# Merging two inverse spectral branches before their shared inverse stage, with SBUF-to-SBUF transfers that turn the rows

## The chip, the cores and the metric

The kernel runs on one core of a Trainium2 chip. The metric is the device time of one execution, in microseconds (us); lower is better. The engines are called PE (TensorE matmul), PEld (its weight loads), DVE (VectorE), ACT (ScalarE), POOL (GpSimd) and SP (SyncE, which here only issues transfers). A profile is one execution, and its span (first to last instruction) is 1.8 us shorter than the time of the same run.

Each timed run has a state: fast, slow (over 1.5% above the fastest of the same kernel), or unknown (a single run). The only profile of the kernel before is of a 155.47 us run, about 1% above the median, so its stage times are good to about 1%.

## The reference

One input `x` (2048 x 1024, bf16) goes through a real 2-D FFT. Its spectrum is multiplied by two sets of complex weights, A and B. Each product is transformed back, and a per-row gate `g` mixes the two.

```python
def _A_ref(x, w_r, w_i):                 # _B_ref is the same with B's weights
    X = rfft2(x.astype(float32), axes=(-2, -1))
    X = X * (w_r + 1j * w_i)
    return irfft2(X, s=(S, D), axes=(-2, -1)).astype(bfloat16)

x = A_x                                  # B_x is not used
g = sigmoid((x * gate_w).sum(-1, keepdims=True))
return g * a + (1 - g) * b               # a, b: the two branches
```

The 2048 rows are treated as 128 x 16 (n1, n2), so that every transform is a matmul with a constant matrix: along n1 (128 points), along n2 (16 points, "the 16-point stage"), and along the 1024 columns ("over d"). The gate depends on the row alone, so it can be folded into the matrix that undoes n1.

## The kernel before

The kernel is written in the form of units ("U") with a reads list and a writes list; a list scheduler in the same file orders them with estimated costs and puts in the semaphore waits. `EV` is an eviction, which copies a PSUM slot (128 x 1024) to SBUF and goes to ACT or DVE, whichever the scheduler thinks is done first.

The stages are: fold of x by symmetry (DVE), forward n1 (PE), gate row (PE), forward over d (PE), forward 16-point stage (PE), then for each branch eight complex products (DVE), the inverse 16-point stage, the inverse over d, and last one mixed inverse over n1, an unfold and a store.

The gate row, whose moving operand is read in runs of 32 elements:

```python
def gate_row(c):
    ops = [mm(misc(0, [[1, 512]], 1), ap(G8, q, [[1, 1]]),
              ap(R3, q * 2048 + c * 32, [[128, 16], [1, 32]]), q == 0, q == 7)
           for q in range(8)]
    ...
```

One product is two multiplies, one subtraction and one addition, for two of the 16 rows kg at once:

```python
def prod(b, m):
    ...
    r = [(tt(ap(RING, TO, ...), x, w, ALU.mult), rd, ["t0"]),
         (tt(ap(RING, TO + 2048, ...), x, ws, ALU.mult), rd, ["t1"])]
    for c, op in enumerate((ALU.subtract, ALU.add)):
        ...
```

The inverse 16-point stage takes the product as the stationary operand, so that the result lands with d on partitions, ready for the inverse over d. That is run once per branch, and each of its 32 results is evicted:

```python
def stage_i1(b, kg):
    ...
    w = ap(PT, p + c * 512 + lb % 2 * 256 + lb // 2, [[2, 128]])       # stationary: data
    r.append(mm(pslot(s, lb * 256, [[1, 256]]), w, ap(KI, z + c * 256, [[1, 256]]), c == 0, c == 1))

def stage_dinv(b, n2):                       # 2 branches x 16 rows n2, 8 matmuls each
    ...
    return U(("di", b, n2), "pe", ops, [("V", b, k) for k in range(16)] + [("Vf", b), "DI"],
             after=[("row", b)] + ([("di", 0, 15)] if b else [("grow", 3)]), slot=True, prio=4,
             then=[lambda s: EV(("evD", b, n2), 1024, dst, pslot(s, 0, [[1, 1024]]), [], w, after=af, slot=s)])

def s1inv(n2):                               # the mixed inverse over n1, from both branches
    ...
```

The weights come in pieces, each for 16 partitions 8g + j, in the order j = 0..3 (`pm` = 0) and then j = 4..7 (`pm` = 1):

```python
for pm in range(2):
    for ii in range(4):
        for c in range(2):
            ...
            prs.append((AP(T, (4 * pm + ii) * P + ..., [[8 * P, 16], [2 * NS, k1 - k0], [1, n]]), ...))
```

Of the kernel before, what the change touches and what calls it, by code (L numbers as in the profile page):

```python
# [10 lines left out]
NS = 514  # L11
PW = 128
# [8 lines left out]
def make_consts():  # L21
# [13 lines left out]
    C["F"] = F.reshape(128, 2048)  # L35
    R = np.zeros((64, 2, 16, 128))
# [4 lines left out]
    C["RM"] = R.reshape(128, 2048)  # L41
# [3 lines left out]
    for h in range(2):  # L45
        d = (h * 128 + np.arange(128))[:, None] + 0.5
        lev, lod = 2 * m, 2 * m + 1
        les = np.where(m == 0, 512, 2 * m)
        DM[:, 0, h] = np.cos(pi2 * lev * d / 1024)
        DM[:, 1, h] = -np.sin(pi2 * lod * d / 1024)  # L50
        DM[:, 2, h] = -np.sin(pi2 * les * d / 1024)
        DM[:, 3, h] = np.cos(pi2 * lod * d / 1024)
# [4 lines left out]
    for par in range(2):  # L57
        for h in range(2):
            l = (2 * (h * 128 + np.arange(128)) + par)[:, None]
            DI[:, par, h, 0] = np.where(l == 0, 1.0, 2.0) / 1024 * np.cos(pi2 * l * d / 1024)  # L60
            li = np.where(l == 0, 512, l)
            DI[:, par, h, 1] = -np.where(li == 512, 1.0, 2.0) / 1024 * np.sin(pi2 * li * d / 1024)
# [3 lines left out]
    KI = np.zeros((2, 2, 128, 2, 16, 4, 2))  # L66
    for z in range(2):
        for pm in range(2):
            for k2 in range(16):
                for ii in range(4):  # L70
# [3 lines left out]
                    for q2 in range(16):  # L74
# [16 lines left out]
                        K = KI[z, :, po, :, q2, i, :]  # L91
# [11 lines left out]
    C["KI"] = KI.reshape(2, 2, 128, 256).transpose(2, 0, 1, 3).reshape(128, 1024)  # L103
# [3 lines left out]
    C["GS"] = np.repeat(gs.reshape(128, 1), 16, axis=1)  # L107
    one = np.zeros((128, 2))
    one[0] = 1.0
    C["ONE"] = one  # L110
    idt = np.zeros((128, 16))
    idt[:16] = np.eye(16)
    C["ID"] = idt
# [13 lines left out]
class Sched:  # L127
# [4 lines left out]
    def __init__(self):  # L132
        self.q = {e: [] for e in self.ENG}
        self.all = []
        self.writer, self.readers = {}, {}
        self.free = {e: 0.0 for e in self.ENG}
        self.dmafree = 0.0

    def ready(self, eng, reads, writes):

        t = self.free[eng]
        for k in list(reads) + list(writes):
            for d in self.writer.get(k, ()):
                t = max(t, d.end + (60 if d.eng == eng else 160))
        for k in writes:
            for d in self.readers.get(k, ()):
                t = max(t, d.end + (0 if d.eng == eng else 160))
        return t

    def op(self, eng, fns, reads=(), writes=(), dma=False, ns=0.0):  # L150
# [10 lines left out]
        for k in writes:  # L161
            o.deps |= self.writer.get(k, set())
            o.deps |= self.readers.get(k, set())
        for k in reads:
# [90 lines left out]
def bass_gated_mix__spectral_gfnet__spectral_gfnet__prompt_kernel(  # L255
# [15 lines left out]
    R2 = sb("R2", 32 * NS)  # L271
    R3 = sb("R3", 16384)
    R4 = sb("R4", 16384)
    R5 = sb("R5", 32 * NS)
    FM = sb("FM", 2048)
    DM = sb("DM", 2048)
    S2 = sb("S2", 768)
    KI = sb("KI", 1024)
    DI = sb("DI", 2048)
    RM = sb("RM", 2048)  # L280
    GS = sb("GS", 16)
    ONE = sb("ONE", 2)
    ID = sb("ID", 16)
    V6 = sb("V6", 256)
    RING = sb("RING", 11264)
    GROW = sb("GROW", 512)
    X5 = sb("X5", 32)
    P5 = sb("P5", 192)
    V5 = sb("V5", 256)
    ZG = sb("ZG", 16)  # L290
    G8 = sb("G8", 8)
# [3 lines left out]
    S = Sched()  # L295
    x2, out2 = A_x[0], out[0]
# [3 lines left out]
    WR = {0: R5, 1: R2}  # L300
    VR = {0: R1, 1: R5}
    QO, TO, PO = 0, 3072, 7168
    VBO, OO, HO, YO = 0, 2048, 4096, 6144
    PSL = [(RING, PO), (RING, PO + 2048), (FM, 0)]

# [6 lines left out]
    def mm(o, l, r, start=True, stop=True):  # L312
        n = int(np.prod(o.shape[1:]))
        return (lambda e: e.matmul(o, l, r, start=start, stop=stop, skip_group_check=True)), max(65.0, 0.42 * n)  # L314
# [13 lines left out]
    class U:  # L328
# [4 lines left out]
        def start(self):  # L333
# [14 lines left out]
            if self.eng == "ev":  # L348
# [3 lines left out]
                return (ta, "act", ca) if ta + ca <= td + cd + (300 if dnext[0] < td + 400 else 0) else (td, "dve", cd)  # L352
# [77 lines left out]
    def cload(eng, t, key, n, alias=(), after=()):  # L430
        return U(("ld", key), eng, [(ap(t, 0, [[1, n]]).bitcast(dt.uint16), cst[key].ap())], [], [key] + list(alias),
# [6 lines left out]
    def wload(b, ka, kb, after=()):  # L438

        prs = []  # L440
        T = WR[b]
        P = pit[id(T)]
        for pm in range(2):
            for ii in range(4):
                for c in range(2):
                    src = wsrc[b][c]
                    n = src.shape[-1]

                    def part(r0, step, k0, k1):
                        prs.append((AP(T, (4 * pm + ii) * P + (2 * k0 + c) * NS, [[8 * P, 16], [2 * NS, k1 - k0], [1, n]]),  # L450
                                    AP(src.tensor, src.offset + (r0 + step * k0) * n, [[128 * n, 16], [step * n, k1 - k0], [1, n]])))
                    if pm == 0:
                        part(16 * ii, 1, ka, kb)
                    elif ii < 3:
                        part(80 + 16 * ii, -1, ka, kb)
                    elif ka == 0:
                        part(128, -1, 1, kb)
                        part(64, 1, 0, 1)
                    else:
                        part(128, -1, ka, kb)  # L460
        return U(("ldw", b, ka), "sp", prs, [], [("W", b, k) for k in range(ka, kb)] + (["gwt"] if b else []),
                 after, dma=(True, 1500.0 * (kb - ka)))

    gwl = U(("ld", "gw"), "act", [(ap(R2, 2048, [[1, 1024]], 0, 1), gate_w.rearrange("(o d) -> o d", o=1))], [], ["gw"],
            dma=(True, 10.0))
    loads = [xload(0, 2), cload("sp", FM, "F", 2048), xload(2, 4), xload(4, 8), xload(8, 12), xload(12, 16),
             cload("sp", DM, "DM", 2048), cload("sp", S2, "S2", 768), cload("sp", KI, "KI", 1024),
             cload("sp", GS, "GS", 16), cload("sp", ID, "ID", 16), wload(0, 0, 8), wload(0, 8, 16),
             wload(1, 0, 16, after=["G8mm"]), cload("sp", DI, "DI", 2048),
             cload("sp", RM, "RM", 2048, ["zrow"], after=["gspec"])]  # L470
# [3 lines left out]
    def fold(name, n, src, soff, tmp, st, dst, doff, p0, np_, reads, skey, writes, eng="dve", after=()):  # L474
# [9 lines left out]
        for i, op in enumerate((ALU.add, ALU.subtract)):  # L484
# [3 lines left out]

    folds = [fold(("fold", m), 2, R1, m * 2048, RING, m % 2 * 2048, R4, m * 2048, 0, 128, [("x", 2 * m), ("x", 2 * m + 1)],
                  ("st", m % 2), [("u", 2 * m), ("u", 2 * m + 1)], after=[("ldx", (0, 2, 4, 4, 8, 8, 12, 12)[m])]) for m in range(8)]  # L490
    gfold = [fold("gfold", 1, R2, 2048, R2, 4096, R2, 3072, 0, 1, ["gw"], ("gst",), [("ug",)], eng="pool", after=[("ld", "gw")])]

    def s1(n2):
        def ops(s):
            return [mm(pslot(s, q * 128, [[1, 128]]), ap(R4, n2 * 1024 + q * 128, [[1, 128]]), ap(FM, n2 * 128, [[1, 128]]))
                    for q in range(8)]
        return U(("s1", n2), "pe", ops, [("u", n2, 0), ("u", n2, 1), "F"], after=[("fold", n2 // 2), ("ld", "F")], slot=True, prio=2,
# [3 lines left out]
    def gate_row(c):  # L501
        ops = [mm(misc(0, [[1, 512]], 1), ap(G8, q, [[1, 1]]), ap(R3, q * 2048 + c * 32, [[128, 16], [1, 32]]), q == 0, q == 7)
               for q in range(8)]
        return U(("grow", c), "pe", ops, ["G8"] + [("Z", 4 * c + i) for i in range(4)], ["m7"], prio=6,
                 after=["G8"] + [("evZ", 4 * c + i) for i in range(4)] + (["x5"] if c == 3 else []),
                 then=[EV(("zrow", c), 512, ap(RM, c * 512, [[8, 16], [128, 4], [1, 8]], 0, 1),
                          misc(0, [[32, 16], [8, 4], [1, 8]], 1), ["m7"], [("zrow", c)])])

    gate = [U("G8mm", "pe", [mm(misc(q, [[1, 1]]), ap(R2, 3072 + q * 128, [[1, 128]], 0, 1), ap(ONE, 0, [[1, 1]], 0, 1))
                             for q in range(8)], [("ug", 0), ("ug", 1), "ONE"], ["m7", "gwt"], after=["gfold", ("ld", "ONE")], prio=6,  # L510
              then=[EV("G8", 8, ap(G8, 0, [[1, 8]]), misc(0, [[1, 8]]), ["m7"], ["G8"])])]
    gate += [gate_row(c) for c in range(4)]
    gate += [U("gspec", "pe", [mm(misc(n2, [[1, 1]]), ap(RM, n2 * 128, [[1, 128]], 0, 1), ap(ONE, 0, [[1, 1]], 0, 1))
                               for n2 in range(16)], [("zrow", c) for c in range(4)] + ["ONE"], ["m7", "zrow"],
# [5 lines left out]
    allu = [("u", m, i) for m in range(16) for i in range(2)]  # L520
# [3 lines left out]
    def stage_d(kg):  # L524
        def ops(s):
            return [mm(pslot(s, o, [[1, 256]]), ap(R3, (2 * g + h) * 2048 + kg * 128, [[1, 128]]),
                       ap(DM, (2 * g + h) * 256, [[1, 256]]), h == 0, h == 1)
                    for g, o in ((0, 0), (3, 256), (2, 512), (1, 768)) for h in range(2)]
        r = kg % 3
        return U(("d", kg), "pe", ops, allz + ["DM"], after=[("evZ", m) for m in range(16)], slot=True, prio=4,  # L530
                 then=[lambda s: EV(("evQ", kg), 1024, ap(RING, QO + r * 1024, [[512, 2], [1, 2], [2, 256]]),
                                    pslot(s, 0, [[512, 2], [256, 2], [1, 256]]), [],
                                    [("Q", r)] + ([("st", i, t) for i in range(2) for t in "ST"] if kg == 0 else []),
                                    after=[("s2", kg - 3)] if kg > 2 else [], slot=s)])

    def stage_s2(kg):
# [3 lines left out]
        def Q(c, a, n):  # L540
            return ap(RING, QO + r * 1024 + c * 512 + a, [[1, n]])

        def ops(s):
# [3 lines left out]
                    mm(pslot(s, 1, [[1, 511]]), Cn, Q(1, 1, 511), False, True),  # L547
                    mm(ap(PS, 3072 + kg, [[1, 1]]), Cn, Q(1, 0, 1)),
                    mm(pslot(s, 513, [[1, 511]]), A, Q(1, 1, 511), False, True),
# [196 lines left out]
```

## Time and profile before

| what | value | from |
|---|---|---|
| time | 154.23 us median (153.45 to 156.2) | three runs |
| span, clock of the PE | 153.7 us, 0.983 | the profiled run |
| DVE / PE / ACT busy | 124.9 / 124.2 / 118.7 us | part 1 of the page |
| first product | 35.72 us | timeline, DVE |
| end of weight traffic | about 68 us | slices, DMA |
| start of branch B's inverse over d | 116.53 us | timeline, PE |
| from there to the end (the tail) | 37.2 us | the same |

The first fence has lines of the profile page of the kernel before: the span, busy time per engine (us, share of the span, instructions), and rows of the span cut into 40 equal slices, in which a digit is the busy share in tenths (the GB/s row is what the transfers moved).

```profile
span 153.7 us, 2554 instructions
PE 124.2 (81%) x1015; PEld 88.4 (58%) x1024; DVE 124.9 (81%) x193; ACT 118.7 (77%) x128; POOL 5.5 (4%) x8
...
DVE  0899998337979989919997996998974699799993
...
PEclk9999999999999999999959999999999999999997
DMA  5899999999999999980000400000000033333253
GB/s 160 272 430 417 307 169 181 177 166 177 175 172 165 164 181 167 167 186 0 0 0 0 138 4 0 0 4 0 0 0 5 0 136 136 136 136 118 95 205 137
```

A slice is 3.84 us. Read the rows by stage. The weights (slices 5 to 17) crawl at about 170 GB/s with the transfer engines full. Almost nothing moves in the middle; stores run at the end. DVE is nearly full from about 35 us on, but for its wait for the last weights in slice 17, and the PE keeps its full clock in all but two slices.

### The profile page before, as it was taken

The numbers are of one execution on the slowest core, as the hardware profiler recorded it, in microseconds if no ns is written. First come the engines' busy times: TensorE is split into PE (matmuls) and PEld (weight loads), VectorE is DVE, ScalarE is ACT, GpSimd is POOL, SyncE is SP. The second block draws the span as 40 slices with busy tenths as digits, with TensorE's granted clock in tenths as the row PEclk, the third lists the DMA queues.
The fourth block names the chain that finished last, engine by engine and source line by source line (L and its number), as shares of the span: only waits on it lengthen the run. The fifth ranks groups of instructions, "written<-read, shape, count | busy, mean of one in ns | idle before, by whom it ended". The sixth has DMA issues, their size and how long they took to land.

```text
span 153.7 us, 2554 instructions
## 1 busy us (share of the span) xinstructions
PE 124.2 (81%) x1015; PEld 88.4 (58%) x1024; DVE 124.9 (81%) x193; ACT 118.7 (77%) x128; POOL 5.5 (4%) x8
## 2 busy tenths in 40 slices
PE   0058897699999999989299599999987999999920
PEld 0057454467686867663168487878876467456400
DVE  0899998337979989919997996998974699799993
ACT  3046889489999899998159689999977789598770
POOL 4900000000000000000000000000000000000000
PEclk9999999999999999999959999999999999999997
DMA  5899999999999999980000400000000033333253
GB/s 160 272 430 417 307 169 181 177 166 177 175 172 165 164 181 167 167 186 0 0 0 0 138 4 0 0 4 0 0 0 5 0 136 136 136 136 118 95 205 137
DMA packets 13422, 19.54 MB, mean 127 GB/s; under 512 B 1761, under 2 KB 10081, under 8 KB 13026
## 3 DMA queue, kind: packets, MB, share of 16 engines
q1 hardware_dynamic: 13264, 19.37, 55.6%
q8 instruction: 8, 0.13, 0.4%
q14 instruction: 4, 0.03, 0.1%
q10 hardware_dynamic: 146, 0.00, 0.1%
HBM read 15.17 MB, written 4.19 MB: 126 GB/s over the span
## 4 chain that ended last, share of the span: by engine, by line
SPq 34%; PE 32%; ACT 10%; DVE 10%; DMA 8%; issue 4%; DVEq 0%
SPq L358 34%; PE PS L314 32%; DVE RING L318 9%; DMA R<-in_B_w_i_dram 8%; ACT R L363 6%; ACT RING L363 3%; DVE FM L318 1%; ACT L363 1%; ACT GROW L363 1%; DVEq L233 0%; DVE P L318 0%; DVE RING L365 0%; DVEq L219 0%
## 5 line engine op out<-in xcount | busy, mean ns | idle before, releaser
L363 ACT ACTIVATE R<-PS 128x1024 bf16<-128x1024 f32 x71 | 68.5, 1030 | 17.2 <-PE PS L314 17.0
L318 DVE TENSOR_TENSOR RING<-R 128x2048 bf16<-128x2048 bf16 (+1 forms) x48 | 49.0, 1062 | 10.7 <-DMA R<-in_A_x_dram 4.3
L363 ACT ACTIVATE RING<-PS 128x1024 bf16<-128x1024 f32 x41 | 43.8, 1131 | 8.3 <-PE PS L314 8.3
L318 DVE TENSOR_TENSOR RING<-RING 128x512 bf16<-128x512 bf16 (+1 forms) x94 | 42.6, 505 | 0.6
L314 PE MATMUL PS<-KI,RING 128*128 128x256 bf16 x240 | 30.4, 279 | 3.1 <-DVE P L318 2.9
L314 PE MATMUL PS<-DI,R 128*128 128x256 bf16 x256 | 30.9, 273 | 1.8 <-ACT R L363 1.8
L314 PEld LDWEIGHTS PS<-DI,R 128*128 128x128 bf16 x256 | 24.2, 98 | 7.5 <-ACT R L363 2.0
L314 PEld LDWEIGHTS PS<-KI,RING 128*128 128x128 bf16 x240 | 22.8, 100 | 8.3 <-issue 3.6
L314 PE MATMUL PS<-FM,R 128*128 128x128 bf16 x128 | 11.1, 250 | 11.8 <-DVE R L318 9.9
L314 PEld LDWEIGHTS PS<-FM,R 128*128 128x128 bf16 x128 | 9.2, 114 | 14.1 <-DVE R L318 8.8
L314 PE MATMUL PS<-RING,S 128*128 128x1 bf16 (+2 forms) x90 | 14.9, 303 | 1.5 <-ACT RING L363 1.2
L314 PE MATMUL PS<-DM,R 128*128 128x256 bf16 x128 | 15.0, 273 | 1.3 <-DVE R L365 1.3
L365 DVE CAST R<-PS 128x1024 bf16<-128x1024 f32 x9 | 11.0, 1223 | 5.9 <-PE PS L314 5.9
L314 PEld LDWEIGHTS PS<-DM,R 128*128 128x128 bf16 x128 | 12.2, 98 | 3.2 <-DVE R L365 1.5
L365 DVE CAST RING<-PS 128x1024 bf16<-128x1024 f32 x7 | 8.7, 1249 | 6.0 <-PE PS L314 6.0
L314 PEld LDWEIGHTS PS<-RING,S 128*128 128x128 bf16 x96 | 7.4, 97 | 8.7 <-ACT RING L363 2.2
L318 DVE TENSOR_TENSOR R<-RING 128x1024 bf16<-128x1024 bf16 x16 | 11.2, 740 | 0.3
L314 PE MATMUL PS<-R,FM 128*128 128x512 bf16 x29 | 8.9, 382 | 2.5 <-ACT RING L363 2.4
L314 PE MATMUL PS<-RING,DM 128*128 128x512 bf16 x32 | 9.5, 379 | 0.0
L314 PE MATMUL PS<-R,G 128*1 128x512 bf16 x32 | 7.5, 378 | 0.0
L314 PEld LDWEIGHTS PS<-R,FM 128*128 128x128 bf16 x32 | 2.6, 97 | 5.9 <-ACT RING L363 4.9
L318 POOL TENSOR_TENSOR R<-R 1x512 bf16<-1x512 bf16 x4 | 5.3, 1336 | 1.9 <-DMA R<-in_gate_w_dram 1.8
(30 smaller groups left out, 33.1 us busy)
## 6 DMA issues: line engine op xcount, KB each, us to landing
out_dram<-RING SPq DMA_DIRECT2D x16, 256.0 KB, 2.0
R<-in_A_x_dram SPq DMA_DIRECT2D x3, 1024.0 KB, 10.7
R<-in_A_w_r_dram SPq DMA_DIRECT2D x15, 128.2 KB, 9.6
R<-in_A_w_i_dram SPq DMA_DIRECT2D x15, 128.2 KB, 9.6
R<-in_B_w_r_dram SPq DMA_DIRECT2D x7, 256.5 KB, 14.5
R<-in_B_w_i_dram SPq DMA_DIRECT2D x7, 256.5 KB, 14.0
R<-in_A_x_dram SPq DMA_DIRECT2D x2, 512.0 KB, 5.1
FM<-c_F SPq DMA_DIRECT2D x1, 512.0 KB, 5.4
```

Source lines behind the costliest of these rows:

```text
L314: return (lambda e: e.matmul(o, l, r, start=start, stop=stop, skip_group_check=True)), max(65.0, 0.42 * n)
L318: return (lambda e: e.tensor_tensor(out=o, in0=a, in1=b, op=op)), 150 + 0.523 * n
L358: S.op(eng, [lambda e, d=d, s=s: e.dma_start(d, s) for d, s in self.ops], self.reads, self.writes, dma=self.dma[0], ns=self.dma[1])
L363: S.op("act", lambda e: e.activation(o, i, f), self.reads, self.writes, ns=x)
L365: S.op("dve", lambda e: e.tensor_copy(o, i), self.reads, self.writes, ns=x)
```

## The change

The intent is to do the inverse n1 transform first and on both branches together, so that they are one before the inverse over d. That halves the inverse over d (128 matmuls in place of 256) and takes away 16 of 32 evictions after it. For this the result of the inverse 16-point stage is needed with n1 on partitions. The 16-point stage now has a fixed matrix as stationary operand, which leaves the result in the wrong layout, and a transfer from SBUF to SBUF ("turn", 256 KB, 32 of them) puts its 128 rows of 2 KB on 8 partitions, 16 rows each.

Along with it came other edits: weights as a common buffer loaded in the order A first half, B first half, A rest, B rest, in pieces that alternate j and j + 4; the spectrum as a ring of four rows; the second step of the fold, for eight of the 16 blocks, moved to the PE; two adds of three products moved to the PE; the l = 512 side path gone; a larger bias of evictions toward ACT; and the gate row rebuilt as small tiled matmuls.

The diff, cut:

```diff
+NX = 4        # rows in the spectrum ring
+NV = 4        # turn buffers
+BIAS = 1200   # was 300: how far ACT is preferred for an eviction
 def gate_row(c):
-    ops = [mm(misc(0, [[1, 512]], 1), ap(G8, q, [[1, 1]]), ap(R3, q * 2048 + c * 32, [[128, 16], [1, 32]]), q == 0, q == 7)
-           for q in range(8)]
+    ops = [mm(ap(PS, 32 * t * 4096 + 7 * 512 + 128 * i, [[1, 128]], 0, 32), ap(VT, 2048 + (4 * r + t) * 32, [[1, 32]]),
+              ap(R3, (4 * r + t) * 2048 + (4 * c + i) * 8, [[512, 4], [1, 8], [128, 4]]), r == 0, r == 1, 32 * t)
+           for i in range(4) for r in range(2) for t in range(4)]
 ...
 def stage_i1(b, kg):
-            w = ap(PT, p + c * 512 + lb % 2 * 256 + lb // 2, [[2, 128]])
-            r.append(mm(pslot(s, lb * 256, [[1, 256]]), w, ap(KI, z + c * 256, [[1, 256]]), c == 0, c == 1))
+    return [mm(pslot(s, 512 * c, [[1, 512]]), ap(KI, k + c * 128, [[1, 128]]), ap(T, t + u0 + u1 + c, [[1, 512]]), ...)
+            for n, (k, u0, u1) in enumerate(w) for c in range(2)]
 ...
+    dm = U(("turn", b, kg), "sp", [(AP(VR[b], (kg % 4 + kg // 4 * 32) * P, [[4 * P, 8], [1024, 16], [1, 1024]]),
+                                    ap(VT, i * 1024, [[1, 1024]]))],
+           [("vt", i)], [("V", b, kg)] + ..., dma=(True, 1300.0), prio=0)
 ...
 def s1inv(n2):
+    return [mm(pslot(s, q * 128, [[1, 128]]), ap(VR[b], n2 * 1024 + q * 128, [[1, 128]]), rb if b else ra, b == 0, b == 1)
+            for q in range(8) for b in range(2)]
+    # needs every turn of both branches: after=[("turn", b, k) for b in range(2) for k in R16]
-def stage_dinv(b, n2):
+def stage_dinv(n2):                    # once, on the merged result
 ...
+    u = U(("ldw", key), "sp", wpiece(...), [], [key] + over(["wpad"] + (wkeys[0, 0] if late else [])), ...)
```

## The prediction

> **What bounds it now.** Page: span 153.7 us; DVE 124.9 busy, ACT 118.7, PE 124.2. No engine is full, so I read it by stage (windows of 4 us, timeline).
> - 0-30 us: x arrives at about 420 GB/s; DVE folds it (32 ops, 22.5 us) until 26.4.
> - 17-67: weights, 8.4 MB in 1026-byte rows, about 170 GB/s with the DMA engines full. The last B row ends DVE's wait at 68.7 (chain of waits).
> - 36-110: DVE does 16 products at a pitch of 3.5 us (multiplies 1.22 x2, adds 0.68 x2).
> - 88-150: inverse over d twice (256 matmuls, 108 ns apart), evictions, mixed inverse, second eviction, unfold (4 x 0.42 us).
> After the weights ACT+DVE are the limit: 128 PSUM evictions, about 1.03 us on ACT, 1.23 on DVE.
>
> **What changes.**
> Removed: 16 evictions (32 after the inverse over d become 16 after the n1 merge), 16.5 us of ACT+DVE; half the inverse-d matmuls (128 x 0.108 = 14 us of PE); the fold's second half for eight of 16 blocks (8 ops of 0.67, 5.4 us of DVE), moved to PE as 64 more 128-column matmuls (0.055 us apart, 3.5 us); the adds of three products (4 us of DVE, moved to PE, 24 matmuls x 0.215 = 5 us); the l=512 side path.
> Added: 32 turns of 256 KB, SBUF to SBUF; 0.5 MB of FN (1.3 us of DMA); a barrier: the n1 merge needs all 32 turns landed. A turn has 8 destination partitions. The Trainium skill, "DMA: Bandwidth & Descriptors", section "Why a DMA increments its semaphore by 16 and not by 1", says the engine count must divide both outer sizes, so 8 of 16 engines. The x load shows 27 GB/s per engine; estimate 1.2 us per turn, 39 us in all, landing 3 us after the eviction. No run shows a turn yet.
> Moved: weights come A first half, B first half, A rest, B rest, because the spectrum is now a ring of four rows that both products must consume; most evictions go to ACT.
>
> **Critical path after.** B's first half lands at about 17 + 12 + 2 (constants) + 12 = 43 us; before that DVE can do only two products. Then 14 products (11 x 3.5 + 3 x 2.3 = 45 us) and 6-7 evictions (8 us) put the last product at 96-98. Two i1 groups (3.5), eviction (1), turn (3): barrier open at 104-107. DMA check: loads 13 + weights 50 + constants 2 + turns 39 = 104 us on the low eight engines, just as tight. Tail: 29 of 32 evictions on ACT, 30 us (PE needs 16 x (0.88 + 0.87) = 28), plus 7-8 for fill, last unfold, store: 37-38. End about 144.
>
> Of 26 us of ACT+DVE work saved (13 each if balanced) I expect 10 to show; the rest goes to the barrier and the DMA.
>
> **Prediction:** 144 us, 8 in 10 between 135 and 152; faster by over 2%: 0.84, within 2%: 0.11, slower: 0.05.
>
> **What would show each step.** Groups: 112 large evictions; 128 inverse-d matmuls instead of 256. DMA issues: 32 turns, landing in 3 us (more under weight traffic). Timeline: third product near 43; a PE gap of 3-5 us before the first n1 merge at 104-107; then ACT over 85% busy. DMA row: busy through 100 instead of ending at 68.
>
> **What would make it wrong.** Turns slower than 1.2 us, or queued behind weights, so that the four turn buffers stall evictions (barrier past 112: about 150). Weight loads wait on products by the shared pad key, so the in-order SP queue may hold both weights and turns. Faster than 135 if the weights stream quicker or DVE idles less than now.

## More of the kernel before

The next lines are from the timelines of the kernel before: start, duration (us), engine, line, operation, output<-input, shape, count, and in brackets the idle time before it and what ended it.

```profile
15.50 1.89 PE L314 MATMUL PS<-R,G 128*1 128x512 bf16 x8
...
68.73 2.36 DVE L318 TENSOR_TENSOR RING<-R 128x2048 bf16<-128x2048 bf16 x2 [3.40 <-DMA R<-in_B_w_i_dram]
...
99.16 1.95 PE L314 MATMUL PS<-KI,RING 128*128 128x256 bf16 x16
100.96 1.95 PE L314 MATMUL PS<-DI,R 128*128 128x256 bf16 x16
...
116.53 2.78 PE L314 MATMUL PS<-DI,R 128*128 128x256 bf16 x24
```

The first is one gate row; the second is DVE's wait of 3.40 us for the last weights. The next two show B's inverse 16-point stage (`KI`) and A's inverse over d (`DI`) taking turns on the PE, so that the two branches overlap. The last is where branch B's inverse over d starts: the 128 matmuls of A's came before it.

## The result, and the profile after

The changed kernel took 173.94 us in the median of four runs (fast: 172.0, 173.82, 174.06; one slow run of 176.84), against 154.21 before. The ratio of times is 1.126, with a 95% interval of 1.113 to 1.138: slower. Ratios here are the mean time of one kernel's fast runs over that of the other's of the same rounds, so not quite the ratio of the medians. The prediction was 144 us, with 0.84 for faster.

The same lines of the page, after (run of 172.0 us; a slice is 4.26 us):

```profile
span 170.2 us, 2841 instructions
PE 129.2 (76%) x1112; PEld 85.2 (50%) x1120; DVE 121.1 (71%) x175; ACT 107.4 (63%) x111; POOL 6.1 (4%) x11
...
DVE  0999972437999295769862999589913039998993
...
PEclk9999999999995699599999999996997599999996
DMA  5999999864412465645554445567254003244353
GB/s 184 359 427 364 274 284 261 229 170 113 114 40 64 114 163 172 225 134 207 151 174 152 124 116 159 173 169 199 68 151 148 24 0 123 99 170 172 123 187 125
```

DVE and ACT together have 15.1 us less work (228.5 against 243.6), yet the span is 16.5 us longer. The work went down and the idle time went up: DVE's row shows gaps that it did not have. The DMA row stays at 4 to 7 tenths from slice 13 to slice 30 (but for one slice), where it had been almost empty from 68 us until the stores. The weights (slices 4 to 7) came at 229 to 284 GB/s, faster than before.

I call "barrier" the first matmul of the merged n1 stage, which needs all 32 turns. These are lines of the timelines of the kernel after (columns as before):

```profile
14.39 3.82 PE L324 MATMUL PS<-R,VT 128*32 128x128 bf16 x32 [1.18 <-ACT R L374]
...
46.95 3.75 PE L324 MATMUL PS<-R,VT 128*32 128x128 bf16 x32
...
133.56 0.29 PE L324 MATMUL PS<-R 128*128 128x128 bf16 x1 [4.23 <-DMA R<-VT]
```

```profile
11.34 7.99 DVE L329 TENSOR_TENSOR R<-R 128x1024 bf16<-128x1024 bf16 x8
...
45.41 5.56 DVE L329 TENSOR_TENSOR TR<-XR,WB 128x2056 bf16<-128x2056 bf16 x2
...
52.03 2.42 DVE L329 TENSOR_TENSOR FM<-XR,WB 128x2056 bf16<-128x2056 bf16 x2
...
119.96 2.37 DVE L329 TENSOR_TENSOR TR<-XR,WB 128x2056 bf16<-128x2056 bf16 x2
```

The two lines with 32 matmuls are gate rows; each takes 3.8 us where the old one took 1.89. While one runs (46.95 to 50.70), DVE's pair of multiplies takes 5.56 us, although such a pair takes 2.37 elsewhere. The third product starts at 52.03 (the prediction said 43), the last one at 119.96 (96 to 98), and the barrier opens at 133.56 (104 to 107). From there the tail takes 36.6 us (37 to 38 predicted): **the whole error lies ahead of the barrier.**

The kernel before needed 37.2 us from the start of B's inverse over d. So the tails are alike, and the change could gain only if its barrier opened before 116.5 us. It opened 17.0 us later, which is nearly all of the 16.5 us by which the span grew.

The end of the chain of waits of the kernel after (start, us, what), followed back from its last instruction, shows what the barrier waited for:

```profile
112.92 6.06 DMA R<-VT
...
119.07 1.03 ACT VT L374
120.12 4.13 DMA R<-VT
...
124.34 1.03 ACT VT L374
...
128.41 5.10 DMA R<-VT
133.51 0.05 issue
133.56 22.03 PE PS L324 x280
```

Turn, eviction into the turn buffer that it freed, turn again: from 112.92 on, transfers make up most of the chain. The windows of the kernel after give the busy time of each engine, the PE clock, the share of the 16 DMA engines and GB/s:

```profile
core 0: us, PE busy (x) PEld busy (x) DVE busy (x) ACT busy (x) POOL busy (x), PEclk, DMA share, GB/s
122.00:124.00 2.00, 1.85 (x13) 0.86 (x11) 1.09 (x3) 0.25 (x1) 0.00 (x0) 1.00 0.50 150
...
130.00:132.00 2.00, 0.00 (x0) 0.00 (x0) 0.85 (x2) 0.02 (x1) 0.00 (x0) 0.50 0.48 148
...
134.00:136.00 2.00, 2.00 (x22) 2.00 (x21) 0.00 (x0) 0.52 (x1) 0.00 (x0) 0.50 0.00 0
```

At 122 to 124 and 130 to 132 only turns are moving. They use half of the engines, as the prediction took from the Trainium skill ("DMA: Bandwidth & Descriptors", section "Why a DMA increments its semaphore by 16 and not by 1"), and the share of 0.50 agrees. (The trace does not number the engines; that they are the low eight is not shown here.) But they move 150 GB/s, about 19 per engine, where the prediction took 27 from the x load. A turn of 256 KB thus needs, as an estimate, 0.262 MB / 150 GB/s = 1.75 us, not 1.2. Over the whole stretch from 121.3 to 133.3, in which the last six turns pass with short lulls, the rate is 132 GB/s at a share of 0.46, or 2.0 us per turn. At 130 to 132 the PE stands still and its clock falls to 0.50, so that the merge (134 to 136) starts at half clock.

### The profile page after: what moved, and what is told of

Same layout as the page of the kernel before. It is cut to its first block, busy times and chain, and to the rows that moved or that the text cites. A ratio compares the mean times of both kernels' runs of the same rounds, so it can differ in the third digit from the quotient of the medians.

```text
span 170.2 us, 2841 instructions
## 1 busy us (share of the span) xinstructions
PE 129.2 (76%) x1112; PEld 85.2 (50%) x1120; DVE 121.1 (71%) x175; ACT 107.4 (63%) x111; POOL 6.1 (4%) x11
## 4 chain that ended last, share of the span: by engine, by line
PE 40%; DMA 18%; DVE 17%; ACT 13%; SPq 5%; issue 4%; DVEq 0%; ACTq 0%
PE PS L324 40%; DMA R<-VT 15%; DVE TR L329 9%; DVE R L329 5%; SPq L369 5%; ACT VT L374 5%; ACT QR L374 4%; ACT R L374 2%; ACT XR L374 2%; DMA R<-in_A_x_dram 2%; DMA WB<-in_B_w_i_dram 2%; DVE FM L329 1%; DVE XR L376 1%; DVE R L376 0%; DVEq L245 0%
## 5 line engine op out<-in xcount | busy, mean ns | idle before, releaser
L374 ACT ACTIVATE R<-PS 128x1024 bf16<-128x1024 f32 x43 | 40.5, 1052 | 19.9 <-PE PS L324 19.9
L324 PE MATMUL PS<-TR,KI 128*128 128x512 bf16 x139 | 37.2, 408 | 13.6 <-DVE TR L329 6.0
L374 ACT ACTIVATE VT<-PS 128x1024 bf16<-128x1024 f32 (+1 forms) x33 | 31.7, 987 | 25.0 <-PE PS L324 13.8
L329 DVE TENSOR_TENSOR TR<-XR,WB 128x2056 bf16<-128x2056 bf16 x30 | 38.7, 1331 | 11.4 <-PE PS L324 4.8
L324 PE MATMUL PS<-DM,R 128*128 128x256 bf16 (+1 forms) x256 | 32.9, 256 | 2.8 <-ACT XR L374 1.8
L329 DVE TENSOR_TENSOR R<-R 128x512 bf16<-128x512 bf16 (+1 forms) x72 | 31.3, 491 | 1.1 <-ACT R L374 0.4
L374 ACT ACTIVATE QR<-PS 128x1024 bf16<-128x1024 f32 x14 | 20.9, 1538 | 5.2 <-PE PS L324 5.2
L324 PE MATMUL PS<-R 128*128 128x128 bf16 x128 | 16.5, 230 | 4.2 <-DMA R<-VT 4.2
L324 PE MATMUL PS<-QR,S 128*128 128x511 bf16 (+2 forms) x93 | 17.2, 317 | 1.9 <-ACT QR L374 1.3
L374 ACT ACTIVATE XR<-PS 128x1024 bf16<-128x1024 f32 (+1 forms) x15 | 11.6, 803 | 6.3 <-DVE FM L329 2.6
L329 DVE TENSOR_TENSOR TR<-TR 128x1028 bf16<-128x1028 bf16 x24 | 15.5, 692 | 0.0
```

The source lines that it names most:

```text
L324: return ((lambda e: e.matmul(o, l, r, start=start, stop=stop, skip_group_check=True, **kw)), max(65.0, 0.42 * n) * (1 if tile is None els ...
L329: return (lambda e: e.tensor_tensor(out=o, in0=a, in1=b, op=op)), 150 + 0.523 * n
L374: S.op("act", lambda e: e.activation(o, i, f), self.reads, self.writes, ns=x)
```

## The experiments

Theory 1 says that the turns are mis-sized and feed back through four turn buffers. Rivals: (2) the rebuilt gate rows delay the start; (3) the weight loads' shared pad key (a name in the scheduler by which a weight load waits for every product issued before it, though they share no bytes) holds the in-order SP queue, so that turns stand behind waits; (4) the ring and the other small buffers stall DVE. All were open at first. The kernel before on the same chip took 154.49 us in the first group (half_turns, gate_runs, pool_turns, no_pad_key), 153.88 in the second (turn16, gate_half, gate_early, before_ports) and 154.28 in the third.

| kernel | time, us | result | third product | last product | barrier |
|---|---|---|---|---|---|
| after | 172.0 (profiled) | right | 52.03 | 119.96 | 133.56 |
| half_turns | 161.74 | wrong | 52.01 | 114.45 | 124.81 |
| gate_runs | 166.31 | right | 43.18 | 114.25 | 127.35 |
| pool_turns | 175.28 | right | 51.66 | 122.80 | 136.16 |
| no_pad_key | 173.58 | right | 52.33 | 119.55 | 134.31 |
| turn16 | 167.2 | wrong | 52.05 | 116.36 | 127.79 |
| gate_half | 154.9 | wrong | 44.15 | 106.43 | 116.36 |
| gate_early | 173.42 | right | 43.13 | 122.28 | 134.86 |
| gate_half_now | 154.97 | wrong | 43.21 | 104.02 | 115.22 |
| ring8 | 150.18 | wrong | 44.14 | 100.52 | 110.46 |

The fast runs of the changed kernel spread over 2 us, so a difference of 1 or 2 us in the time column says nothing. Inside the trace, the first product starts at 40.30 to 40.97 us in the runs with the old gate rows and at 34.82 to 35.84 us in those with gate_runs' edit, so a shift of 1 us at a mark says nothing either.

### half_turns: turns of half the bytes

```diff
-[[4 * P, 8], [1024, 16], [1, 1024]]),  ap(VT, i * 1024, [[1, 1024]])
+[[4 * P, 8], [1024,  8], [1, 1024]]),  ap(VT, i * 1024, [[1, 1024]], 0, 64)
```

> The changed kernel, but each turn moves only half of its rows (64 of 2 KB instead of 128), same issues in the same order; the result is wrong on purpose. Theory T (the turns saturate the low eight DMA engines: 32 x 1.7 us = 55 us of the 75 us between the first turn and the barrier): the barrier before the first n1 merge, now at 133.5 us, comes at 105 to 118 and the total falls to 145 to 158 us. Rival S (the in-order SP queue and the waits of weight loads on products hold the pipeline, not bytes): barrier stays above 126, total above 166. Rival L (fixed landing latency with four turn buffers): in between, 160 to 166, because the fixed part of a landing stays.

Only 64 of 128 rows are moved, so the output is wrong; the instruction order stays. The barrier moves from 133.56 to 124.81, the time by 10 us. The third product stays at 52. ACT's waits for a free turn buffer nearly vanish. This is their line in the waits (waited-for us in total, times, longest), first of the kernel after, then of half_turns:

```profile
ACT VT L374 <- DMA R<-VT: 11.2, 6, 5.4
```

```profile
ACT VT L374 <- DMA R<-VT: 0.5, 1, 0.5
```

One half turn alone has this window (columns as above):

```profile
115.10:116.10 1.00, 1.00 (x4) 0.34 (x3) 1.00 (x2) 0.37 (x1) 0.00 (x0) 0.50 0.44 119
```

At 119 GB/s its 0.131 MB take 1.1 us, close to the 1.2 that was predicted for a whole turn. So the mis-sized turn is worth most of the 8.7 us at the barrier. The time and the barrier fell short of what theory T expected; 161.74 lies in the range given to rival L, in which a fixed part of each landing stays. No run separates that part.

### gate_runs: the same gate rows, read in runs

```diff
-    mm(ap(PS, ..., [[1, 128]], 0, 32), ..., ap(R3, ..., [[512, 4], [1, 8], [128, 4]]), ...)
+    mm(ap(PS, ..., [[32, 4], [1, 4], [4, 8]], 0, 32), ..., ap(R3, ..., [[512, 4], [128, 4], [1, 8]]), ...)
```

> The changed kernel with one difference: the 128 matmuls of the gate rows read their moving operand in runs of 8 elements instead of single elements 256 bytes apart, and write PSUM in the permuted order instead. Same instructions, same order, right result. Theory G (the strided moving read makes these matmuls slow and blocks the VectorE and ScalarE instructions that run beside them): 32 of them take under 2.5 us instead of 3.8, the eight half folds fall from 1.06 us on average to about 0.7, the mean of the ScalarE evictions into QR from 1.54 to 1.32, the first product starts near 36 instead of 40.6, the first turn near 48 to 53 instead of 58.6; the total falls by 3 to 10 us. Rival (the column tiling itself is slow): nothing changes by more than 1 us.

The moving operand was read one element at a time, 256 bytes apart. Now its innermost dimension is a run of 8 elements, and the turning-around is left to the PSUM side. The same numbers are computed in the same instruction order. Timeline lines of gate_runs, PE, then DVE and ACT:

```profile
25.77 1.06 PE L324 MATMUL PS<-R,VT 128*32 128x128 bf16 x32
...
11.92 4.99 DVE L329 TENSOR_TENSOR R<-R 128x1024 bf16<-128x1024 bf16 x8 [0.56 <-DMA R<-in_A_x_dram]
...
39.68 2.38 DVE L329 TENSOR_TENSOR TR<-XR,WB 128x2056 bf16<-128x2056 bf16 x2
...
43.18 2.36 DVE L329 TENSOR_TENSOR FM<-XR,WB 128x2056 bf16<-128x2056 bf16 x2
...
41.30 1.35 ACT L374 ACTIVATE QR<-PS 128x1024 bf16<-128x1024 f32 x1 [2.02 <-PE PS L324]
```

For the last of these, the kernel after has this line of ACT's timeline, beside its last gate row:

```profile
47.02 4.37 ACT L374 ACTIVATE QR<-PS 128x1024 bf16<-128x1024 f32 x1 [2.02 <-PE PS L324]
```

A gate row falls from 3.8 to 1.06 us, the eight folds from 7.99 to 4.99, the multiply pair from 5.56 to 2.38, the eviction from 4.37 to 1.35. The read pattern of a matmul slowed the PE, and DVE and ACT stood nearly still for as long. The scattered side is now the PSUM write, and whatever that costs is within the 1.06 us; so it was the SBUF read. GpSimd can't be behind it: its last instruction in the kernel after ends at 7.5 us. The Trainium skill, "SBUF — State Buffer", section "Specifications (TRN2)", says that crossing to a new 16-byte line costs a penalty; it agrees in kind, without a size. The same page, section "SBUF: two separate sides", says "PE, ACT, and DVE's dedicated pair never wait on anyone"; these lines speak against it.

The third product comes 8.9 us earlier, the barrier 6.2, and the time falls to 166.3. The rest of the 8.9 is lost again in the turns.

### pool_turns: turns issued by POOL

```diff
-dm = U(("turn", b, kg), "sp", ...
+dm = U(("turn", b, kg), "pool", ...
```

> The changed kernel with all 32 turns issued from GpSimd instead of SP. Theory T: if this path spreads the turns over all 16 DMA engines the barrier comes 10 to 25 us earlier; if they stay on eight it moves by less than 5 us. Rival S (in-order SP queue): the weights of B's second half no longer sit behind turns, so the DVE wait of 4.6 us for them goes, and the total falls by 5 to 15 us even if the DMA engines in use are the same. If issuing from GpSimd costs several us per turn, it gets slower.

No gain: 175.28. After the last product, where turns run alone, the windows of pool_turns (columns as above) have the DMA share at about a half as well:

```profile
128.00:130.00 2.00, 2.00 (x11) 0.87 (x9) 0.85 (x2) 1.17 (x2) 0.55 (x1) 1.00 0.54 135
```

The landing takes 5.3 us in the median. DVE's wait for B's later weights fell from 4.64 to 1.24 us, which did not help either. So a queue of their own did not bring the turns in earlier, and the share gives no sign that one turn got more engines from another issuer.

### no_pad_key: weight loads without the shared key

```diff
-u = U(..., [], [key] + over(["wpad"] + (wkeys[0, 0] if late else [])),
+u = U(..., ["wpad"], [key] + over(wkeys[0, 0] if late else []),
```

> The changed kernel, but a weight load depends on the memset of the pad columns only, no longer on every product issued before it (they share no bytes). Rival S: the SP queue's 12.5 us of waits for products vanish, the A and B weights are all in earlier, the first turn is issued up to 3 us earlier, total 5 to 12 us less. Theory T: total changes by less than 4 us, since the engines that the turns use stay the limit.

The prediction had named this key as a danger. The wait was real, and harmless. These are lines of SP's waits in the queue, first of the kernel after, then of no_pad_key:

```profile
SPq L369 <- DVE TR L329: 12.5, 7, 4.9
```

```profile
SPq L369 <- DVE TR L329: 0.9, 2, 0.5
```

The wait fell by 11.6 us, and the time stayed (173.58). SP then waited for ACT's evictions instead (29.9 us, 16.0 in the kernel after). Rival 3 falls.

### turn16: all 16 engines for a turn

```diff
-AP(VR[b], (kg % 4 + kg // 4 * 32) * P, [[4 * P,  8], [1024, 16], [1, 1024]])
+AP(VR[b], kg % 8 * P + kg // 8 * 8192, [[8 * P, 16], [1024,  8], [1, 1024]])
```

> The changed kernel, each turn with the same 128 rows of 2 KB, but to 16 destination partitions with 8 rows each instead of 8 with 16; the result is wrong on purpose. Theory T-engines (eight of 16 DMA engines carry a turn): the DMA share while only turns run goes from 0.50 to about 1, a turn takes 0.9 to 1.2 us instead of 1.75, the barrier comes at 123 to 128 (half_turns had 124.8), total 160 to 165. Rival T-ports (the destination's write ports bound it; this pattern still writes eight groups): share near 1 but the rate stays near 150 GB/s, and the total near 172.

The rows go to wrong places (wrong output), 16 partitions 8 apart, 8 rows each. The barrier moves by 5.8 us to 127.79. But the rate did not double; these are windows of turn16 after its last product. The first holds one turn alone:

```profile
118.55:119.95 1.40, 1.40 (x11) 0.71 (x9) 0.94 (x3) 1.26 (x2) 0.00 (x0) 0.96 0.72 187
120.00:122.00 2.00, 2.00 (x10) 0.87 (x9) 0.85 (x2) 1.55 (x3) 0.00 (x0) 1.00 0.66 163
122.00:124.00 2.00, 1.25 (x9) 0.60 (x7) 0.00 (x0) 0.68 (x2) 0.00 (x0) 1.00 0.57 151
```

The 2 us windows have gaps between turns (from 118.20 to 118.55, say, nothing moves), so their 163 and 151 GB/s are not the rate of one turn. Alone, a turn passes within 1.4 us: less than the 1.75 us with eight destination partitions, but not half. The barrier is in the range of theory T-engines, the share, the turn and the total are not; rival T-ports has the total wrong too. With half_turns (1.1 us per turn, 8.7 us at the barrier) this brackets a turn of the predicted 1.2 us: as an estimate, 6 to 9 us at the barrier.

By the port formula of the Trainium skill ("SBUF — State Buffer", section "Door 1: The DMA port swizzle (why `[64,N]` ≈ `[32,N]`)") partitions 8 apart reach only 8 of 16 ports, so 16 engines may have met there. No run separates that from other limits. In the right layout one turn (128 rows, 16 for each partition) has only 8 destination partitions; turning two rows kg at once would give it 16, which was not tried.

### gate_half: both together

The edits of gate_runs and half_turns.

> The changed kernel with both gate_runs and half_turns; wrong result on purpose. If the slow gate rows (start of the products, 9 us) and the bytes of the turns (9 us) are two separate causes that hide each other in part: third product at 43, barrier at 114 to 119, total 149 to 154. If the turns' bytes are the same limit that both relieve: total no lower than 158. What is then left over the predicted barrier at 104-107 is waits for weights, product buffers and the spectrum ring (10 to 12 us).

The time is 154.9, the barrier 116.36. Gate alone gave 6.2 us at the barrier, turns alone 8.7, both 17.2. They do not share a cause; together they give a little more than their sum. Even with turns of half the bytes, which the right kernel can't have, the changed kernel only ties with the one before. Something else still lies in its product phase. Lines of DVE's timeline of gate_half:

```profile
50.89 2.37 DVE L329 TENSOR_TENSOR TR<-XR,WB 128x2056 bf16<-128x2056 bf16 x2 [3.01 <-PE PS L324]
...
80.13 2.37 DVE L329 TENSOR_TENSOR TR<-XR,WB 128x2056 bf16<-128x2056 bf16 x2 [3.28 <-DMA WB<-in_B_w_i_dram]
```

From the third product to the last, DVE's waits of this kind add up to 10.4 us in gate_half (3.01, 1.20, 0.68, 3.28, 0.24, 0.92, 0.42 and 0.68). The prediction had none.

### gate_early: weights issued as early as they can

The edits of gate_runs and no_pad_key, and no throttle on B's later weights:

```diff
-        if b and ka:          # hold B's later weights back until the queue is short
+        if False:
```

> The changed kernel with gate_runs, the pad key removed, and B's second half of weights issued as soon as their columns are free, most of them before the first turn, instead of interleaved with turns; right result. Theory: the DVE wait for weights (4.6 us in the changed kernel, 5.7 in gate_runs) goes, and the low DMA engines do weights while they would otherwise be idle at 40-48 us; barrier at 119 to 124 against 127.4 of gate_runs, total 158 to 163. If turns alone are the limit, total stays at 165 to 167.

I had expected 158 to 163; it took 173.42, worse than gate_runs (166.31). Its line of the waits for turn buffers:

```profile
ACT VT L374 <- DMA R<-VT: 20.6, 10, 7.9
```

The waits for turn buffers doubled against gate_runs (10.1; 11.2 in the kernel after). The schedule also moved: turns came in batches. I read this as weights ahead of turns in one queue, but the two effects were not taken apart. Since no_pad_key alone changed nothing, the missing throttle is the likelier of the two edits to blame; it was not tested alone.

### gate_half_now: no second-half weights of B

```diff
-    ... + w[18:] + wseq([(1, 8, 12), (1, 12, 16)])
+    ... + w[18:]                       # B's rows 8 to 15 read the weights of rows 0 to 7
```

> The changed kernel with gate_runs, half_turns, and no weights for the second half of B (its products read those of the first half); wrong result on purpose. Takes away 2.1 MB of weight traffic and 32 issues that share the queue with the turns. gate_half left 10.4 us of VectorE waits between the third product and the last. If those are mostly waits on weights and on the shared queue: barrier at 108 to 111 us (116.4 in gate_half), total 145 to 149. If they are the ring of four spectrum rows and the three product buffers handing over between PE, ScalarE and VectorE: barrier at 112 to 116, total 150 to 155.

On top of gate_half, 2.1 MB of loads fall away (output wrong). The barrier moves by 1.1 us, 0.9 of which is there at the third product already, so it is within the scatter, and the time stays (154.97). The 3.28 us wait for weights is gone, and in its place DVE waits 1.91 and 0.50 us for the PE at 78 to 81 us: late weights were not what held the products.

### ring8: a spectrum ring of eight rows

```diff
-NX = 4
+NX = 8
-WB = sb("WB", 28 * 2 * NS)
+WB = sb("WB", 24 * 2 * NS)             # room for the ring; there are no B second-half weights here
```

> gate_half_now with the ring of spectrum rows eight long instead of four (the space comes from the weights that it does not load); wrong result on purpose. Theory R (the ring makes the evictions of later spectrum rows wait for both products of earlier ones, and PE, which runs in order, waits behind them): ScalarE's 2.5 us wait on the third product and VectorE's 3 us wait on PE near 47-50 go, barrier at 107 to 112 us instead of 115.2, total 145 to 150. Rival (three product buffers, four turn buffers and three PSUM slots hand over slowly whatever the ring): barrier above 113, total above 152.

On top of gate_half_now: barrier 110.46, 4.8 us earlier (although its first product starts 0.9 us later), time 150.18. Of DVE's waits between the third product and the last one large one is left (the others are under 1.4 us), in this line of its timeline:

```profile
88.72 1.23 DVE L376 CAST XR<-PS 128x1024 bf16<-128x1024 f32 x1 [4.93 <-PE PS L324]
```

So the ring of four rows costs about 5 us. In the code it ties A's products to B's, and the evictions of the forward stage to both. The last 5 us to the predicted barrier (104 to 107) stay open: this wait says what was waited for, not which buffer was behind it.

### before_ports: the old kernel with the new order of the weight pieces

```diff
-for pm in range(2):
-    for ii in range(4):
-        for c in range(2):
+for ii in range(4):
+    for c in range(2):
+        for pm in range(2):
```

> The kernel before, with only the order of its weight loads changed: pieces for partitions 8g+j and 8g+j+4 alternate, as in the changed kernel, instead of all j below 4 first. Theory P (consecutive pieces that write only every second group of four partitions share half of the write ports, hence 170 GB/s before and 260-285 after): weights stream at 240 GB/s or more, the last B row lands at 48 to 54 us instead of 67, VectorE's wait of 3.4 us at 68.7 goes, total 1 to 4 per cent less than before (149 to 153 us). Rival (the faster rate of the changed kernel has another cause): rate and total stay.

The page of before_ports:

```profile
DMA  5999999789999992000001300000000052333153
GB/s 143 314 421 421 328 276 269 192 206 208 207 209 211 211 220 74 0 0 4 0 0 19 126 0 0 0 4 0 0 1 4 0 193 93 132 144 140 73 209 139
```

With pieces j and j + 4 in turn, the weights run at about 208 GB/s where they had run at 170, and end near 58 us instead of 68 (240 or more and 48 to 54 us had been expected). By the same formula of the skill the pieces j = 0..3 reach 8 of the 16 ports and j = 4..7 the other 8, so the measurement agrees in direction. The total is the same: 152.95 us against 153.88, ratio 0.997 (0.989 to 1.004). The weights looked like the bound of the old kernel (DVE waited 3.40 us for them); in before_ports that wait is gone and the time is the same, so they were not.

### before_fold and before_fold5: what the change has without its merge

before_fold is before_ports with the half fold on the PE and an eviction bias of 1200; before_fold5 has a bias of 500.

```diff
-(300 if dnext[0] < td + 400 else 0)
+(1200 if dnext[0] < td + 400 else 0)     # before_fold5: 500
+    # in both: half_fold, FN and the doubled forward n1 matmuls, as in the change
```

> A version meant to beat both: the kernel before with the parts of the change that cost no barrier: alternating weight pieces (before_ports), the half fold of eight blocks (8 VectorE operations of 0.67 us less, 64 more 128-column matmuls), and the bias that sends evictions to ScalarE while a VectorE operation is ready (1200 instead of 300). VectorE is over 95% busy from 36 to 64 and from 68 to 92 us of the kernel before, so theory V (VectorE bounds the middle) expects 3 to 8 us less: 146 to 151 us. Rival (ScalarE and VectorE evictions together bound it, so moving evictions to ScalarE only moves the wait): 151 to 156 us.

> As before_fold, with a weaker bias (500), so that VectorE keeps more evictions. Theory V expects this to lie between before_ports (153) and before_fold; if balance matters more than VectorE's own load it is the better of the two, 146 to 150 us.

before_fold took 153.01 us against 154.28, ratio 0.993 (0.986 to 1.000): within 2%, and hardly a gain. That is in the range of the rival (151 to 156), not of theory V. before_fold5 took 160.48, ratio 1.038 (1.028 to 1.048): slower, where 146 to 153 had been expected, and from before_fold it differs in the bias alone. Its ACT waits far more on the PE:

```profile
ACT RING L364 <- PE PS L315: 13.9, 12, 6.5
```

In before_fold the same wait is 3.4 us, in the kernel before 8.3. The bias steers a list scheduler, and the order that comes of it moves the time by over 7 us, more than the edits it was meant to serve. No version was found that beats the kernel before by 2%.

## Why the prediction was wrong

**What was right.** The tail: 36.6 us, 37 to 38 predicted, with a PE gap of 4.23 us before it (3 to 5) and ACT 92% busy in it from 136 to 164 us (over 85). Turns on 8 of 16 engines: share 0.50. The counts: 112 large evictions, 128 matmuls in the inverse over d. These are lines of the groups, before and then after:

```profile
L314 PE MATMUL PS<-DI,R 128*128 128x256 bf16 x256 | 30.9, 273 | 1.8 <-ACT R L363 1.8
```

```profile
L324 PE MATMUL PS<-QR,R 128*128 128x256 bf16 x128 | 15.0, 273 | 1.3 <-ACT R L374 1.3
```

The saving of work was right too: in gate_runs, DVE and ACT are busy 220.1 us together, 23.5 less than before; the prediction said 26.

**Steps that failed.** All of them add up ahead of the barrier, 133.56 in place of 104 to 107, about 28 us.

1. "Third product near 43." It came at 52.03. The rebuilt gate row was never costed, though it stood in the diff. It takes 3.8 us and freezes DVE and ACT; read in runs (gate_runs), the third product comes at 43.18. That alone is worth 6.2 us at the barrier.
2. "Estimate 1.2 us per turn, 39 us in all." It took the rate per engine from a load of x; turns move 19 GB/s per engine, so 1.75 us and 56 us in all (estimates from that rate). Halving them, to 1.1 us each, is worth 8.7 us at the barrier alone, 11.0 once the gate rows are cured (127.35 to 116.36). The mechanism in "What would make it wrong" (turns slower, four buffers stalling evictions) is the one that happened, but it had been given a small chance.
3. "Then 14 products ... put the last product at 96-98." That sum had no idle time of DVE in it. With both faults above cured, the last product still starts at 106.43 (the prediction's sum gives its end, so the gap is wider than it looks). Removing B's late weights brings the barrier only 1.1 us forward, which is within the scatter, and doubling the ring 4.8 us, to 110.46, with the last product at 100.52. About 5 us to the predicted barrier stay open.

As a sum at the barrier: 17.2 us (gate rows and turns together), 1.1 (weights), 4.8 (ring), 5 open, 28.1 in all. The 17.2 includes turns that are a little faster than the prediction's (1.1 against 1.2 us), so it is the upper end of that share, and the 1.1 is no more than the scatter between runs.

**An error the other way.** "B's first half lands at about 43 us" was drawn from the old 170 GB/s. The weights came at 229 to 284 GB/s; before_ports shows that the alternating order of the pieces raises the rate by itself (170 to 208 in the old kernel), though not that it is the whole difference. In gate_runs the third product follows the one before it without any wait for weights. So 43 was a right number for a wrong reason. It helped nothing, as before_ports shows for the old kernel.

**The missed judgement.** Both kernels have the same tail, so the change gains only if all of both branches is through the turns before 116.5 us, when the old kernel starts B's inverse over d. The old kernel does A's inverse over d under B's products; the merge gives that overlap up, since it starts only when the last turn has landed. Comparing the two marks would have shown a margin of 10 to 12 us (116.5 less 104 to 107) that rested on three unproven terms, and 0.84 was far too sure.

## What to carry to other kernels

When a change trades work for a barrier, compare the time at which the barrier opens with the time at which the old kernel starts the same last stretch: work saved on engines that then idle ahead of the barrier buys nothing. Cost every operation that the diff rewrites, also the small ones, and look at the stride of the innermost dimension of matmul operands: 32 small matmuls with scattered reads held three engines for 3.8 us. Take the rate of a transfer from one of its own kind and direction, and give a phase with small rings a measured idle share, not zero.

## What the Trainium skill lacked or had wrong

- "SBUF — State Buffer", section "SBUF: two separate sides", says that PE, ACT and DVE's dedicated pair never wait on anyone. While matmuls read SBUF one element at a time, 256 bytes apart, a DVE multiply pair took 5.56 us (2.38 with runs of 8 elements) and an ACT eviction 4.37 us (1.35).
- The same page, section "Specifications (TRN2)", tells of a penalty for crossing 16-byte lines without a size. For a bf16 moving operand of 128 columns in four column tiles, 32 matmuls took 3.8 us with every element in another line and 1.06 us with runs of 8.
- "DMA: Bandwidth & Descriptors" gives a rate per engine of about 27 GiB/s and says, in section "Where 436 GB/s comes from", that 435 GB/s is what binds between SBUF and SBUF; it has no measured rate of a plain local copy. Copies of 128 rows of 2 KB onto 8 partitions moved about 19 GB/s per engine (150 GB/s on 8 engines); the x load here moved 27 (430 GB/s on 16).
